# Second weight's conversion a step sooner, raw words two turns ahead, and k, q and v of batches 1 to 7 loaded from GpSimd's queue

## The chip, the cores and the metric

One core of a Trainium2 chip runs the kernel. The metric is the time of one execution in microseconds (us) on the device, lower is better. The kernel before was timed in three runs: 1645.82, 1646.19 and 1647.7, median 1646.19.

## The reference

```python
# q, k, v: (8 batches, 8 heads, 576 rows, 64), float32
q_s = softmax over the 64 features of each row of q
k_s = softmax over the 576 rows of each feature of k
kv  = einsum('bhsd,bhse->bhde', k_s, v)
att = einsum('bhsd,bhde->bhse', q_s, kv)
x = att.transpose(0, 2, 1, 3).reshape(4608, 512)
h = np.maximum(x @ w_in, 0.0)           # w_in 512 x 2048, w_out 2048 x 512
x = h * h @ w_out                       # first layer
h = x @ w_in2                           # second layer, own weights
out = (h / (1 + np.exp(-h))) @ w_out2   # silu
```

The four weights arrive as float64. q, k and v are float32.

## The kernel before

**Weights.** A float64 weight is read as raw 64-bit words (`raw`, loaded by `load_w`, L128 and L133, two DMAs a tile) and turned to float32 by hand (`to_f32`): ACT makes two activations (L143, L144), DVE four steps (L145, L148, L149, L152). Each weight has 8 tiles of 128 x 1024. Products are made in three matmuls from operands split in a high and a low half (`split`: ACT casts the high half at L117, DVE subtracts for the low half at L118; `mm3`, L187 to L189, gives high x high, high x low, low x high).

**Attention.** A `Pair` is two heads of one batch, 32 in all. `load` sets the padding of kr by a GpSimd memset (L241) and loads k (two DMAs, L235 and L239) and q (two: L235 and L239 for batches 0 and 1, L248 after them); `load_v` sets v's columns and padding by memsets (L257, L258) and loads v (three DMAs, L261 twice, L264). `k_max` takes the maximum on DVE (km, m: L269 to L271) and, across partitions, on GpSimd (L275, into mb); `k_sub` (L281) subtracts it, after which the buffer kr is free for the next pair's memset and load; `k_exp` (L288) is on ACT, `kv` (L296) and the transposed q times kv (`x`, matmuls named xp) on PE. For batches 2 to 7, q's own steps are `q_max` (L336 to L338), the exponential (L341), `q_norm` (L358 to L362), a transpose on DVE (L375) and the split of q into qh and ql.

**Prologue.** Batch 0's four pairs (`early`) run first, one step after the other in a loop over i, with loads on SP's and ACT's queues. `conv_first` converts the first tile of w_in (o = 0) and of w_out (o = 1); its generator is advanced once at step i = 2, and `run(conv)` takes the rest after the loop. The second of these, named w, feeds the first w_out product (matmuls named op). Its halves are the casts of `u` at L117 and L118.

**First layer.** Block 0 (512 tokens) goes through 16 steps f: hp = x @ w_in (L643), `relu2` (L632, L633) and the split into g, and op matmuls with w. Blocks 1 to 8 (j) take 8 turns each (m, one for each double tile i of the weights). A turn makes x @ w_in by a Strassen product of seven parts (matmuls L589, into a and c; additions at L601 to L624 on ACT and DVE into h), and the op matmuls of the turn before. Hooks in a turn advance the attention of the remaining 28 pairs (batches 1 to 7) by a phase. In the last turn of each j, `x_first` makes x for the next block (xt, L528 to L531, and the split in L118). SP loads in each turn the halves wah and wal of the weights' sums (L497).

**Second layer's weights.** `prepare` loads raw words of a tile (a step), converts them in the next step, and sends the result to DRAM (`wf`); from j = 2 on it is advanced in turns 0 to 5. After about 750 us the second layer begins: 6 steps of 8 turns.

**What sets the order.** Tile buffers are recycled: a pool tile with a tag (kr, v, q, mb) has one buffer, and the 19 large slots (`take`, `give`) are handed on in the order in which they come free. A scheduler orders the instructions of each engine by its own costs, so the order on an engine is not the order of the source. Each engine, and SP's and POOL's queue among them, runs its row in order. SP issues all loads but those early ones that ACT issues.

Of the kernel before, what the change touches and what calls it, by code (L numbers as in the profile page):

```python
# [11 lines left out]
U32 = mybir.dt.uint32  # L12
# [8 lines left out]
P = 128  # L21
# [9 lines left out]
def kernel(  # L31
# [13 lines left out]
    nc = tc.nc  # L45
    B, H, S, D = q.shape
# [4 lines left out]
    SM = S // TB * TB  # L51
    SL = S - SM
    NB = NT // TB
    SC = SM // P
# [7 lines left out]
    NP = NF // 2  # L62
# [4 lines left out]
    upool = ctx.enter_context(tc.tile_pool(name="u", bufs=2))  # L67
# [12 lines left out]
    def take(shape, dt, name):  # L80

        at = idle.pop(0)
        t = spool.tile(shape, dt, tag=f"s{at}", name=name)
        slot_of[id(t)] = (at, t)
        return t

    def give(*tiles):
        for t in tiles:
            idle.append(slot_of.pop(id(t))[0])

    def f32(t):
        return t.bitcast(F32)
# [18 lines left out]
    PW = 2 * NK * P  # L111
    wf = dpool.tile([2, NP, 2, P, PW], F32, name="wf")
# [8 lines left out]
    def load_w(l, i, o):  # L121

        raw = take([P, PW], U64, "raw")
        for e in range(2):
            f = slice((2 * i + e) * P, (2 * i + e + 1) * P)
            r = raw[:, e * NK * P:(e + 1) * NK * P]
            if o == 0:
                nc.sync.dma_start(  # L128
                    out=r.rearrange("p (k f) -> p k f", k=NK),
                    in_=(w_in1, w_in2)[l][:, f].rearrange("(k p) f -> p k f", p=P),  # L130
                )
            else:
                nc.sync.dma_start(out=r, in_=(w_out1, w_out2)[l][f, :])  # L133
        return raw

    def to_f32(u, raw, pin=False):

        words = raw.bitcast(U32).rearrange("p (n two) -> p n two", two=2)  # L140
        lo32, hi32 = words[:, :, 0], words[:, :, 1]
        keep = tc.keep_in_program_order if pin else lambda r: r
        keep(nc.scalar.activation(f32(lo32), lo32, AF.Copy, scale=2.0 ** -51, bias=2.0))  # L143
        keep(nc.scalar.activation(f32(u), f32(hi32), AF.Abs))  # L144
        nc.vector.tensor_scalar(  # L145
            out=f32(u), in0=f32(u), scalar1=EXP_LO, scalar2=EXP_HI, op0=ALU.max, op1=ALU.min
        )
        nc.vector.tensor_scalar(out=u, in0=u, scalar1=3, scalar2=None, op0=ALU.logical_shift_left)  # L148
        nc.vector.scalar_tensor_tensor(  # L149
            out=u, in0=hi32, scalar=0x80000000, in1=u, op0=ALU.bitwise_and, op1=ALU.bitwise_xor  # L150
        )
        nc.vector.tensor_tensor(out=u, in0=u, in1=lo32, op=ALU.add)  # L152
# [16 lines left out]

    def prepare():  # L170

        for i in range(NP):
            for o in range(2):
                raw = load_w(1, i, o)
                yield
                u = upool.tile([P, PW], U32, tag="u", name="u")
                to_f32(u, raw)
                give(raw)
                nc.sync.dma_start(out=wf[1, i, o], in_=f32(u))
                yield  # L180

    def run(steps):
# [18 lines left out]
    class Pair:  # L201
# [27 lines left out]
        def load(self):  # L229
            b, h0 = self.b, 2 * self.p  # L230
            self.kr = self.tile("kr", [P, 2, SC + 1, D], F32)
            self.q = self.tile("q", [P, 2, SC + 1, D] if self.natural else [P, S32, 32], F32)

            def rows(t, src, queue):
                queue.dma_start(  # L235
                    out=t[:, :, 0:SC].rearrange("p a c d -> p a (c d)"),
                    in_=src[b, h0:h0 + 2, 0:SM].rearrange("h (p c) d -> p h (c d)", p=P),
                )
                queue.dma_start(out=t[0:SL, :, SC], in_=src[b, h0:h0 + 2, SM:S].rearrange("h p d -> p h d"))  # L239

            nc.gpsimd.memset(self.kr[SL:P, :, SC], LEAST)  # L241
            rows(self.kr, k, nc.sync)
            if self.natural:
                nc.gpsimd.memset(self.q[SL:P, :, SC], 0.0)
                rows(self.q, q, nc.scalar if self.early else nc.sync)
            else:
                for dh in range(2):
                    nc.sync.dma_start(  # L248
                        out=self.q[64 * dh:64 * dh + 64],
                        in_=q[b, h0:h0 + 2, :, 32 * dh:32 * dh + 32].rearrange("h (s c) d -> (h s) c d", c=S32),  # L250
                    )

        def load_v(self):

            b, h0 = self.b, 2 * self.p
            self.v = self.tile("v", [P, SC + 1, 2, D + 1], F32)
            nc.gpsimd.memset(self.v[:, :, :, D:], 1.0)  # L257
            nc.gpsimd.memset(self.v[SL:P, SC, :, 0:D], 0.0)  # L258
            vv = self.v[:, :, :, 0:D]
            for a in range(2):  # L260
                nc.sync.dma_start(  # L261
                    out=vv[:, 0:SC, a], in_=v[b, h0 + a, 0:SM].rearrange("(p c) d -> p c d", p=P)
                )
            nc.sync.dma_start(out=vv[0:SL, SC], in_=v[b, h0:h0 + 2, SM:S].rearrange("h p d -> p h d"))  # L264

        def k_max(self):
            m = self.tile("m", [P, 2, D], F32)
# [363 lines left out]
    def relu2(h, src):  # L631
        nc.scalar.activation(h, src, AF.Relu)  # L632
        nc.scalar.activation(h, h, AF.Square)  # L633
        g = gpool.tile([P, 2, TB], F32R, tag="g", name="g")
        split(g[:, 0], g[:, 1], h)
        return g
# [93 lines left out]
    for i in range(NK + 2):  # L730
        a = early[i] if i < NK else None
        b = early[i - 1] if 1 <= i <= NK else None
        c = early[i - 2] if 2 <= i else None
        if a:
            a.q_exp()
            a.k_sub()
        if b:
            b.kv()
            b.q_norm()
            b.q_t()  # L740
        if i + 1 < NK:
            early[i + 1].k_max()
            early[i + 1].q_max()
        if b:
            b.kv_evac()
            b.q_split()
        if a:
            a.k_exp()
        if c:
            c.x_evac()  # L750
        if b:
            b.x()
        if i == 2:
            next(conv)
    run(conv)
    ahead = prepare()
# [30 lines left out]
    for j in range(1, NB):  # L787
        x, xs = xs, None
        for m, i in enumerate(turns[j - 1]):
            def hook(n):  # L790
                if (j, m, n) == (1, 0, 3):
                    wa.want(0)
                if n in (1, 6):
                    next(attend, None)
                    if j == 1 and (m, n) in ((1, 6), (3, 6)):
                        next(attend, None)
                if j < NB - 1:
                    if m == 4 and n == 0 and j == NB - 2:
                        XR[j + 1] = take([P, NK, TB], F32, "xr")
                        nc.sync.dma_start(out=XR[j + 1], in_=xld.rearrange("k p t -> p k t"))  # L800
                    if m == NP - 1:
                        if n == 0:
                            state["x"] = x_first(j + 1)
                            state["x"].split(2)
                        elif n == 4:
                            x.done(4)
                            state["x"].split(2)
                        elif n == 7:
                            x.done(NQ)
                            state["x"].split(3)  # L810
                else:
                    if m == 4 and n == 0:
                        state["raw"] = load_second(0)
                    elif m == 5 and n == 0:
                        state["x"] = x_second(state["raw"])
                        state["x"].split(2)
                    elif m == 6 and n == 0:
                        state["x"].split(1)
                    elif m == 7 and n == 0:
                        state["x"].split(1)  # L820
                    elif m == 7 and n == 4:
                        x.done(4)
                        state["x"].split(2)
                    elif m == 7 and n == 7:
                        x.done(NQ)
                        state["x"].split(1)

            state = {} if m == 0 else state
            h = hpool.tile([P, 2, TB], F32, tag="h", name="h")
            g = strassen(wa.tiles[0, i], x.x, TB // 2, h, lambda v: relu2(v, v), hook, (2, 2, 2))  # L830
            before = out_pair(j, m, i, g)
            t += 1
            wa.want(t)

            if j >= 2 and m < 6:
                next(ahead, None)
        xs = state["x"]
    run(ahead)
# [36 lines left out]
    for s in range(STEPS):  # L875
        x, state = xs, {}
        for m, i in enumerate(turns[NB - 1 + s]):
# [16 lines left out]
            h = lpool.tile([P, 2, TS], F32, tag="h", name="h")  # L894
# [37 lines left out]
```

## Time and profile before

| what | value |
|---|---|
| three runs | 1645.82, 1646.19, 1647.7 us |
| profiled execution, its own time | 1645.36 us |
| its span in the profile | 1643.5 us |
| granted TensorE clock, mean | 0.997 |
| ACT busy | 858.7 us (52%) |
| SP's queue (q1): packets, MB, share of 16 engines' span | 191152, 317.50, 58.2% |

The profile is of one execution. Busy times are sums over all instructions of an engine; PE is the matmul unit, PEld its weight load, DVE the vector engine, ACT the scalar engine, POOL GpSimd, SP the engine that issues most DMAs (SPq is its queue). A row of the time line is: start in us, duration, engine, line, operation, out<-in, shapes, count, and in brackets the idle time ahead of it with what ended it. A row by stretches of time is: the stretch and its length, busy time and count for PE, PEld, DVE, ACT and POOL, the granted clock of PE, the busy share of the DMA engines, GB/s. A row of waits is: engine, what waited, what for, then sum, count and longest. A row of groups gives the count, then the busy sum and mean ns of one, then the idle time ahead by what ended it. A row of DMA issues ends with the size and the median time from issue to landing.

### The profile page before, as it was taken

Reading aid. Unit: us, or ns where it says so; the run is one execution under the profiler, and the core shown is the slowest. Engines: PE = TensorE matmul, PEld = TensorE weight load, DVE = VectorE, ACT = ScalarE, POOL = GpSimd, SP = SyncE. Lnnn points to the kernel's source line nnn. Section 1 sums busy time; section 2 is a strip of 40 time slices with the busy share of each in tenths; the row PEclk is TensorE's granted clock in tenths of the full one; section 3 lists DMA queues with packets and bytes.
Section 4 is the critical chain, followed back from the end, with each engine's and each line's share of the span. In section 5 each row is a group of like instructions: output and inputs, shape, how many; then the busy total and the mean of one; then the engine's idle time right before and its main releaser. Section 6 shows DMA issues by size and latency. Waiting matters only on the chain.

```text
span 1643.5 us, 24901 instructions
## 1 busy us (share of the span) xinstructions
PE 1598.5 (97%) x9624; PEld 1394.2 (85%) x9624; DVE 979.3 (60%) x1708; ACT 858.7 (52%) x1529; POOL 55.4 (3%) x149
## 2 busy tenths in 40 slices
PE   4999999999999999999999999999999999999998
PEld 3567888888888888889998888998998998998997
DVE  7998896877858686643336765435435435435333
ACT  5866676666656665564556544324334334334332
POOL 2010000001000000000000000000000000000000
PEclk9999999999999999999999999999999999999999
DMA  8856767778685867554446875444444454454521
GB/s 258 285 161 201 232 201 236 224 244 243 172 266 153 256 207 240 191 192 167 159 164 246 325 277 186 158 170 170 150 180 168 143 189 165 136 205 161 180 95 39
DMA packets 193511, 320.41 MB, mean 195 GB/s; under 512 B 113264, under 2 KB 142960, under 8 KB 188528
## 3 DMA queue, kind: packets, MB, share of 16 engines
q1 hardware_dynamic: 191152, 317.50, 58.2%
q8 instruction: 76, 1.25, 0.3%
q10 hardware_dynamic: 2240, 1.31, 0.3%
q14 instruction: 43, 0.35, 0.1%
HBM read 248.51 MB, written 70.25 MB: 194 GB/s over the span
## 4 chain that ended last, share of the span: by engine, by line
PE 72%; DMA 5%; ACT 4%; DVE 3%; issue 1%; SPq 0%; POOL 0%; DVEq 0%; ACTq 0%; POOLq 0%
PE a L589 19%; PE c L589 14%; PE y L188 8%; PE y L189 8%; PE y L187 8%; PE op L188 5%; PE op L189 5%; PE op L187 5%; DMA raw<-in_moe_w_in_dram 2%; DMA raw<-in_moe_w_out_dram 2%; ACT h L632 1%; ACT raw L143 1%; ACT h L633 1%; PE xp L187 1%; DMA x1d<-o 0%
## 5 line engine op out<-in xcount | busy, mean ns | idle before, releaser
L589 PE MATMUL a<-x,wah 128*128 128x256 f32 (+1 forms) x1792 | 394.2, 307 | 5.6 <-ACT h L624 2.7
L589 PEld LDWEIGHTS a<-x,wah 128*128 128x128 f32 x1792 | 311.3, 189 | 36.6 <-ACT h L624 6.4
L589 PE MATMUL c<-x,wah 128*128 128x256 f32 (+1 forms) x1344 | 294.4, 306 | 1.9 <-DVE h L611 1.2
L589 PE MATMUL a<-x,wal 128*128 128x256 f32 (+1 forms) x896 | 273.9, 306 | 0.0
L187 PE MATMUL op<-g,w 128*128 128x512 f32 x576 | 231.0, 404 | 5.5 <-ACT w L117 5.4
L188 PE MATMUL op<-g,w 128*128 128x512 f32 x576 | 228.7, 397 | 0.3 <-DVE g L118 0.3
L589 PEld LDWEIGHTS c<-x,wah 128*128 128x128 f32 x1344 | 224.0, 190 | 3.7 <-DVE h L611 1.7
L189 PE MATMUL op<-g,w 128*128 128x512 f32 x576 | 225.7, 392 | 0.0
L189 PE MATMUL y<-wb,g 128*128 128x512 f32 x576 | 225.0, 391 | 0.0
L188 PE MATMUL y<-wb,g 128*128 128x512 f32 x576 | 224.8, 390 | 0.0
L187 PE MATMUL y<-wb,g 128*128 128x512 f32 x576 | 223.6, 390 | 0.5 <-ACT wb L117 0.5
L589 PE MATMUL c<-x,wal 128*128 128x256 f32 (+1 forms) x672 | 205.1, 305 | 0.0
L611 DVE TENSOR_TENSOR h<-c,h 128x256 f32<-128x256 f32 (+1 forms) x112 | 53.6, 478 | 250.4 <-PE c L589 248.8
L589 PEld LDWEIGHTS a<-x,wal 128*128 128x128 f32 x896 | 169.0, 189 | 0.6 <-DVE wal L118 0.6
L866 ACT ACTIVATE z<-h 128x768 f32<-128x768 f32 x96 | 80.5, 846 | 133.4 <-DVE h L619 132.3
L632 ACT ACTIVATE h<-h 128x512 f32<-128x512 f32 x128 | 80.9, 632 | 105.9 <-DVE h L619 104.8
L118 DVE TENSOR_TENSOR g<-h,g 128x512 fp32r<-128x512 f32 x128 | 88.3, 690 | 78.9 <-ACT g L117 78.5
L189 PEld LDWEIGHTS op<-g,w 128*128 128x128 f32 x576 | 108.9, 189 | 24.0 <-DVE w L118 0.5
L187 PEld LDWEIGHTS op<-g,w 128*128 128x128 f32 x576 | 109.6, 191 | 21.9 <-ACT w L117 5.5
L589 PEld LDWEIGHTS c<-x,wal 128*128 128x128 f32 x672 | 127.6, 190 | 0.0
L189 PEld LDWEIGHTS y<-wb,g 128*128 128x128 f32 x576 | 108.1, 188 | 22.4
L187 PEld LDWEIGHTS y<-wb,g 128*128 128x128 f32 x576 | 108.1, 188 | 22.0 <-ACT wb L117 0.8
(153 smaller groups left out, 2179.8 us busy)
## 6 DMA issues: line engine op xcount, KB each, us to landing
wah<-wad SPq DMA_DIRECT2D x72, 896.0 KB, 6.5
wal<-wad SPq DMA_DIRECT2D x72, 896.0 KB, 6.0
wb<-wbd SPq DMA_DIRECT2D x30, 1024.0 KB, 4.8
raw<-in_moe_w_in_dram SPq DMA_DIRECT2D x32, 512.0 KB, 5.9
raw<-in_moe_w_out_dram SPq DMA_DIRECT2D x32, 512.0 KB, 4.8
wad<-wah SPq DMA_DIRECT2D x16, 896.0 KB, 3.7
wad<-wal SPq DMA_DIRECT2D x16, 896.0 KB, 4.5
x1d<-o SPq DMA_DIRECT2D x18, 512.0 KB, 4.6
```

The costliest lines, as they stand in the source:

```text
L118: nc.vector.tensor_sub(lo, src, f32(hi))
L143: keep(nc.scalar.activation(f32(lo32), lo32, AF.Copy, scale=2.0 ** -51, bias=2.0))
L187: nc.tensor.matmul(ps, lh, rh, start=first, stop=False)
L188: nc.tensor.matmul(ps, lh, rl, start=False, stop=False)
L189: nc.tensor.matmul(ps, ll, rh, start=False, stop=last)
L589: nc.tensor.matmul(ps, l, r, start=first and c == 0 and n == 0, stop=c == 1 and n == 2, skip_group_check=True)
L611: nc.vector.tensor_add(h[:, 0, two], c, h[:, 0, two])
L632: nc.scalar.activation(h, src, AF.Relu)
L633: nc.scalar.activation(h, h, AF.Square)
L866: nc.scalar.activation(z, h, AF.Sigmoid)
```

## The change

Three edits. First, the generator of `conv_first` is advanced at step 3 of the prologue too, so the raw words of the first w_out tile are converted a step sooner. Second, `prepare` goes in groups of three tiles: the raw words of the next are loaded before those of the one ahead are converted, and the generator is advanced in turns 0, 2, 4 and 6 in place of 0 to 5. So a tile is converted two turns after its load, and up to two raw tiles are held. Third, k, q and v of batches 1 to 7 are issued by GpSimd: seven DMAs a pair, 196 in all, in place of SP. Lines after the diff's first piece have numbers that are 3 higher, and 4 higher from L261 on.

```diff
     def prepare():
-        for i in range(NP):
-            for o in range(2):
-                raw = load_w(1, i, o)
-                yield
-                u = upool.tile([P, PW], U32, tag="u", name="u")
-                to_f32(u, raw)
-                give(raw)
-                nc.sync.dma_start(out=wf[1, i, o], in_=f32(u))
+        todo = [(i, o) for i in range(NP) for o in range(2)]
+        for at in range(0, len(todo), 3):
+            raw = None
+            for i, o in todo[at:at + 3] + [(None, None)]:
+                done, raw = raw, None if i is None else (i, o, load_w(1, i, o))
+                if done:
+                    u = upool.tile([P, PW], U32, tag="u", name="u")
+                    to_f32(u, done[2])
+                    give(done[2])
+                    nc.sync.dma_start(out=wf[1, done[0], done[1]], in_=f32(u))
                 yield
...
-            rows(self.kr, k, nc.sync)
+            rows(self.kr, k, nc.sync if self.early else nc.gpsimd)
...
-                rows(self.q, q, nc.scalar if self.early else nc.sync)
+                rows(self.q, q, nc.scalar if self.early else nc.gpsimd)
             else:
                 for dh in range(2):
-                    nc.sync.dma_start(
+                    nc.gpsimd.dma_start(
...
+            queue = nc.sync if self.early else nc.gpsimd
             for a in range(2):
-                nc.sync.dma_start(
+                queue.dma_start(
...
-            nc.sync.dma_start(out=vv[0:SL, SC], ...)
+            queue.dma_start(out=vv[0:SL, SC], ...)
...
-        if i == 2:
+        if 2 <= i <= 3:
             next(conv)
...
-            if j >= 2 and m < 6:
+            if j >= 2 and m % 2 == 0:
                 next(ahead, None)
```

**DVE at the end of the prologue.** The rows below are those around the first split of g, which the first op matmuls need. u_380 is the buffer of the second weight before the change, u_340 the same after it; k_453 belongs to the first later pair, km_618 (from kr_523) to the second. Before:

```order
L281 TENSOR_TENSOR k_453<-kr_401,mb_420 128x640
L145 TENSOR_SCALAR u_380<-u_380 128x1024
L329 TENSOR_REDUCE qm_422<-q_402 128x10
L148 TENSOR_SCALAR u_380<-u_380 128x1024
L332 TENSOR_TENSOR q_402<-q_402,qm_422 128x640
L149 SCALAR_TENSOR_TENSOR u_380<-raw_157,u_380 128x1024
L118 TENSOR_TENSOR g_398<-r_395,g_398 128x512
L152 ISA u_380<-raw_157,u_380 128x2048
L344 TENSOR_REDUCE qs_426<-q_402 128x10
L145 TENSOR_SCALAR w32_434<-w32_434 128x1024
L118 TENSOR_TENSOR g_450<-r_447,g_450 128x512
L118 TENSOR_TENSOR w_387<-u_380,w_387 128x1024
```

After:

```order
L285 TENSOR_TENSOR k_453<-kr_401,mb_420 128x640
L118 TENSOR_TENSOR w_387<-u_340,w_387 128x1024
L336 TENSOR_TENSOR q_402<-q_402,qm_422 128x640
L145 TENSOR_SCALAR u_476<-u_476 128x1024
L148 TENSOR_SCALAR u_476<-u_476 128x1024
L307 TENSOR_SCALAR rec_518<-kvp_497 128x1
L273 TENSOR_TENSOR km_618<-kr_523 128x256
L149 SCALAR_TENSOR_TENSOR u_476<-raw_163,u_476 128x1024
L118 TENSOR_TENSOR g_398<-r_395,g_398 128x512
L348 TENSOR_REDUCE qs_426<-q_402 128x10
L152 ISA u_476<-raw_163,u_476 128x2048
```

The second weight's conversion (L145 to L152) has gone from between L281 and the splits to places ahead of these rows; its low half (w_387) is now made right behind the first later pair's subtraction. The low half of g_398 stands behind the km of the second later pair, which it stood ahead of.

**ACT at the same place.** r_395 is the first relu2, g_398 its high half. Before:

```order
L144 ACTIVATE u_380<-raw_157 128x1024
L632 ACTIVATE r_395<-hp_390 128x512
L288 ACTIVATE k_453<-k_453 128x640
L633 ACTIVATE r_395<-r_395 128x512
L632 ACTIVATE r_447<-hp_442 128x512
L117 CAST g_398<-r_395 128x512
L633 ACTIVATE r_447<-r_447 128x512
L341 ACTIVATE q_402<-q_402 128x640
L143 ACTIVATE raw_160<-raw_160 128x1024
L144 ACTIVATE w32_434<-raw_160 128x1024
L117 CAST g_450<-r_447 128x512
L117 CAST w_387<-u_380 128x1024
```

After:

```order
L144 ACTIVATE u_476<-raw_163 128x1024
L117 CAST w_387<-u_340 128x1024
L410 COPY xr_99<-xp_379 128x288
L410 COPY xr_99<-xp_381 128x224
L413 COPY big_126<-xp_381 128x64
L292 ACTIVATE k_453<-k_453 128x640
L414 DMA xld_95<-big_126 128x64
L636 ACTIVATE r_395<-hp_390 128x512
L143 ACTIVATE raw_428<-raw_428 128x1024
L637 ACTIVATE r_395<-r_395 128x512
L345 ACTIVATE q_402<-q_402 128x640
L117 CAST g_398<-r_395 128x512
```

The second weight's two activations (L143 and L144 of raw_157) and its high half (w_387) now stand ahead of the last early pair's x block; L143 of other raw words (raw_428) stands between the two activations of the first relu2.

**PE at the same place.** The first op matmuls; op0 to op3 are the four blocks of the result. Before:

```order
L296 MATMUL kvp_497<-v_409,k_453 64x65 x10
L187 MATMUL op0_460<-g_398,w_387 128x512
L188 MATMUL op0_460<-g_398,w_387 128x512
L187 MATMUL op1_464<-g_398,w_387 128x512
L189 MATMUL op0_460<-g_398,w_387 128x512
L188 MATMUL op1_464<-g_398,w_387 128x512
L189 MATMUL op1_464<-g_398,w_387 128x512
L187 MATMUL op2_468<-g_398,w_387 128x512
L188 MATMUL op2_468<-g_398,w_387 128x512
```

After:

```order
L300 MATMUL kvp_497<-v_409,k_453 64x65 x10
L190 MATMUL op0_460<-g_398,w_387 128x512
L190 MATMUL op1_464<-g_398,w_387 128x512
L190 MATMUL op2_468<-g_398,w_387 128x512
L190 MATMUL op3_472<-g_398,w_387 128x512
L191 MATMUL op0_460<-g_398,w_387 128x512
L192 MATMUL op0_460<-g_398,w_387 128x512
L191 MATMUL op1_464<-g_398,w_387 128x512
L192 MATMUL op1_464<-g_398,w_387 128x512
```

The four high x high matmuls now stand together ahead of those that need a low half.

**GpSimd in a turn.** One pair of batches 2 to 7, from a kr memset to the next. Before:

```order
L241 MEMSET kr 64x2x64
L257 MEMSET v 128x10
L258 MEMSET v 64x2x64
L275 ISA mb<-m 128x128
L241 MEMSET kr 64x2x64
```

After:

```order
L244 MEMSET kr 64x2x64
L238 DMA kr<-in_k_dram 128x2x256
L242 DMA kr<-in_k_dram 64x2x64
L251 DMA q<-in_q_dram 64x18x32 x2
L260 MEMSET v 128x10
L261 MEMSET v 64x2x64
L265 DMA v<-in_v_dram 128x4x64 x2
L268 DMA v<-in_v_dram 64x2x64
L279 ISA mb<-m 128x128
L244 MEMSET kr 64x2x64
```

All seven DMAs of the pair now stand in this row, v's three between the memsets of v and the next pair's all-reduce.

**DVE in the turn in which x is split.** One such turn, from the pair's subtraction to the next pair's km. Before:

```order
L281 TENSOR_TENSOR k<-kr,mb 128x640
L615 TENSOR_TENSOR h<-a,h 128x256
L358 TENSOR_REDUCE qs<-q 128x18
L619 TENSOR_TENSOR h<-c,h 128x256
L321 COPY qsu<-qs 64x18
L322 COPY qsu<-qs 64x18
L360 SCALAR_TENSOR_TENSOR qs<-qs,qsu 128x18
L361 RECIPROCAL qs<-qs 128x18
L362 TENSOR_TENSOR q<-q,qs 128x576
L269 TENSOR_TENSOR km<-kr 128x256
```

After:

```order
L285 TENSOR_TENSOR k<-kr,mb 128x640
L619 TENSOR_TENSOR h<-a,h 128x256
L118 TENSOR_TENSOR ql<-qt,qh 128x576
L623 TENSOR_TENSOR h<-c,h 128x256
L379 STREAM_TRANSPOSE qt<-q 128x576
L273 TENSOR_TENSOR km<-kr 128x256
```

The next pair's km has moved up: q's sum and normalization no longer stand between the subtraction and it.

More of the change, by code (lines that the diff above doesn't have):

```diff
@@ L259, in load_v @@
             vv = self.v[:, :, :, 0:D]
+            queue = nc.sync if self.early else nc.gpsimd
             for a in range(2):
-                nc.sync.dma_start(
+                queue.dma_start(
                     out=vv[:, 0:SC, a], in_=v[b, h0 + a, 0:SM].rearrange("(p c) d -> p c d", p=P)
                 )
-            nc.sync.dma_start(out=vv[0:SL, SC], in_=v[b, h0:h0 + 2, SM:S].rearrange("h p d -> p h d"))
+            queue.dma_start(out=vv[0:SL, SC], in_=v[b, h0:h0 + 2, SM:S].rearrange("h p d -> p h d"))
         def k_max(self):
```

## Prediction

> **What bounds the kernel now.** I read the page first, then the busy table by stretches of time, then what PE waited for, then the time line around each of those waits.
>
> ```profile
> PE 1598.5 (97%) x9624; PEld 1394.2 (85%) x9624; DVE 979.3 (60%) x1708; ACT 858.7 (52%) x1529; POOL 55.4 (3%) x149
> ...
> 20.00:40.00 20.00, 16.72 (x121) 10.00 (x121) 15.09 (x36) 14.25 (x32) 1.73 (x4) 1.00 0.91 289
> 40.00:60.00 20.00, 14.89 (x43) 9.48 (x44) 20.00 (x28) 17.27 (x22) 0.84 (x2) 0.83 0.91 286
> ...
> 1600.00:1643.50 43.50, 38.48 (x188) 33.84 (x187) 12.91 (x17) 11.88 (x19) 0.00 (x0) 0.98 0.10 37
> ```
>
> PE is the bound: its idle time is 1643.5 - 1598.5 = 45.0 us of the span, 5.0 of it (43.50 - 38.48) at the very end. The change touches nothing after the first layer (about 750 us), so it can only win PE's holes before that, and the clock where a hole costs it. In 40 to 60 the granted clock is 0.83. The holes by cause:
>
> ```profile
> DVE h L611 <- PE c L589: 248.8, 68, 6.5
> ...
> ACT raw L143 <- DMA raw<-in_moe_w_in_dram: 18.2, 7, 4.2
> ...
> PE kvp L296 <- ACT big L341: 16.7, 1, 16.7
> ...
> DVE k L281 <- POOL mb L275: 12.5, 19, 0.9
> DVE km L269 <- DMA kr<-in_k_dram: 12.1, 7, 3.2
> ...
> PE op L187 <- ACT w L117: 5.4, 1, 5.4
> PE xp L187 <- ACT kvh L117: 5.3, 6, 1.2
> ...
> PE a L589 <- ACT h L624: 2.7, 5, 0.9
> ```
>
> Each row names who waits for whom, then the sum, the count and the longest. Of PE's four, the 16.7 us is the first attention pair before any matmul; its loads stay on SP and ACT. The 5.4 is the wait for the second weight, the 5.3 and 2.7 lie in the turns. ACT and DVE wait for raw words and for k; whether PE pays is seen only at each place.
>
> **Part 1, the second weight's conversion.** Its steps (L143, L144 on ACT, L145 to L152 on DVE, the two halves by L117, L118) end ahead of the first w_out1 matmul:
>
> ```profile
> 30.68 0.43 SPq L235 DMA_DIRECT2D kr<-in_k_dram  x1
> 31.18 0.34 DVE L306 SCALAR_TENSOR_TENSOR big<-kvp,big,mask_n 128x128 f32<-128x128 f32 x1
> 32.79 0.58 ACT L380 COPY big<-qt 128x512 f32<-128x512 f32 x1 [3.07 <-PE qt L369]
> 34.70 0.42 DVE L269 TENSOR_TENSOR km<-kr 128x256 f32<-128x256 f32 x1 [3.18 <-DMA kr<-in_k_dram]
> 36.61 0.82 DVE L281 TENSOR_TENSOR k<-kr,mb 128x640 f32<-128x640 f32 x1 [0.83 <-POOL mb L275]
> 36.64 1.15 ACT L144 ACTIVATE u<-raw 128x1024 f32<-128x1024 f32 x1
> 37.69 0.57 ACT L632 ACTIVATE r<-hp 128x512 f32<-128x512 f32 x1
> 44.01 1.05 ACT L117 CAST w<-u 128x1024 fp32r<-128x1024 f32 x1
> 45.11 0.80 PE L187 MATMUL op<-g,w 128*128 128x512 f32 x1 [5.37 <-ACT w L117]
> ...
> 44.00:46.00 2.00, 0.89 (x2) 0.80 (x3) 2.00 (x4) 2.00 (x3) 0.00 (x0) 0.51 1.23 252
> ...
> 48.00:50.00 2.00, 2.00 (x6) 1.60 (x5) 2.00 (x3) 2.00 (x3) 0.00 (x0) 0.50 0.25 79
> 50.00:55.00 5.00, 5.00 (x15) 2.70 (x15) 5.00 (x9) 2.43 (x3) 0.64 (x1) 0.91 0.74 210
> ...
> L145 DVE TENSOR_SCALAR u<-u 128x1024 f32<-128x1024 f32 x24 | 16.6, 691 | 18.0 <-ACT u L144 18.0
> L152 DVE CUSTOM_DVE_ANT_0 u<-raw,u 128x2048 uint16<-128x2048 uint16 x24 | 29.3, 1223 | 0.0
> ```
>
> PE stands 5.37 us and then runs at half clock from 45.1 to about 50.9 (0.91 over the 5 us from 50 is 0.9 us at a half): (50.9 - 45.1) x 0.5 = 2.9 us more. So this place holds 5.4 + 2.9 = 8.3 us, and no more. The room for the earlier conversion is there: ACT is idle 3.07 us ahead of 32.79 and DVE 3.18 ahead of 34.70. The conversion takes 2 x 1.15 = 2.3 us of ACT and, with each of its four DVE steps at one of the last two rows (two at 0.69, two at 1.22), 3.8 us of DVE. It is not free, for DVE's queue now has those 3.8 us ahead of the last pair's L306 (before, it ended at 31.5). That ends near 31.5 + 3.8 = 35.3, and the x block and the first hp matmul need it. The first relu2 (L632) could then start at about 38, as now. But ACT's queue now puts L143, L633, L341 and the cast of g behind it: 38 + 0.57 + 1.15 + three steps of about 0.65 = 41.7. So the four hi-hi matmuls that now open PE's row can start at 41.7 instead of 45.1.
>
> The next matmul, L188, wants the low half of g. In DVE's new row that stands behind the L269 of the second later pair, and so behind that pair's load of k, which GpSimd may issue only when L281 of the pair ahead has read the buffer. L281 stays near 36.6 to 37.4. With 0.2 us for the memset, one issue (about 1 us, below) and a landing of 4.0 (30.68 to 34.70, the load that L269 waited for here), L269 runs at 42.6, and after it stand 0.4 + 1.2 + 0.7 us: low half at 44.9. PE then stops from 42.7 to 44.9. It has done 4 of the 12 matmuls by then and goes on 0.2 us ahead of before, with 0.9 us of work in hand: 1.1 us gained. The clock is not told by a row: a hole of 5.37 gave 0.50, and here there are two of about 2. I take half of its 2.9. Part 1: -1.1 - 1.5 = -2.6, between -8.3 (nothing waits) and +2 (the load of k lands 5 us later, as at 368.97 below, and the clock falls as before).
>
> The Trainium skill, "TensorE: Matmul & The Clock Gate", Part 1: The HAM clock gate, says that the array falls to half rate after about one idle window of some 3.4 us. By it two holes of about 2 us keep full rate, and Part 1 would be -4.0 instead of -2.6; the 0.50 after 5.37 us agrees with it.
>
> **Part 2, k, q and v on GpSimd's queue, and raw words earlier.** The six waits of PE's xp matmul are four of 1.19 us (4.76 of the 5.3), at like places of four j in a row, and two of some 0.25. The first of the four:
>
> ```profile
> 361.52 0.83 DVE L281 TENSOR_TENSOR k<-kr,mb 128x640 f32<-128x640 f32 x1 [0.91 <-POOL mb L275]
> ...
> 367.76 1.11 SPq L128 DMA_DIRECT2D raw<-in_moe_w_in_dram  x2
> 368.97 0.46 SPq L235 DMA_DIRECT2D kr<-in_k_dram  x1
> 374.96 1.16 ACT L143 ACTIVATE raw<-raw 128x1024 f32<-128x1024 uint32 x1 [1.78 <-DMA raw<-in_moe_w_in_dram]
> 376.10 0.43 DVE L269 TENSOR_TENSOR km<-kr 128x256 f32<-128x256 f32 x1 [2.07 <-DMA kr<-in_k_dram]
> 383.63 0.40 PE L187 MATMUL xp<-qh,kvh 128*128 128x288 f32 x1 [1.19 <-ACT kvh L117]
> ...
> 368.97 7.11 DMA kr<-in_k_dram
> ```
>
> SP issues k only at 368.97, behind the raw words and what they waited for, though L281 had read the buffer by 361.52 + 0.83 = 362.3; it lands 7.11 us later. DVE stands 2.07 us, then has the conversion and the kv block to do, and PE's xp matmul comes 1.19 us late. On GpSimd k goes out at about 362.6, so it is in place by 370, and the raw words have two more turns: both waits end, what is next is DVE's own work, and 4 x 1.19 = 4.8 us of PE are free. The other holes of the turns (L624 2.7, the two small xp waits 0.5) I leave as they are: a floor of 0 and a top of 4.8 + 3.2 = 8.0.
>
> What is added is GpSimd's time and the order on it. No row shows a DMA issued by POOL. POOL is in order: in each of 28 pairs 7 issues (k 2, q 2, v 3) now stand there, v's three between the memset that waits for the kv matmuls and the all-reduce of the next pair's maximum.
>
> ```profile
> L275 POOL PARTITION_ALL_REDUCE mb<-m x28 | 29.1, 1039 | 175.0 <-DVE m L271 163.2 <-DVE qs L360 8.7 <-DVE qm L337 3.1
> L258 POOL MEMSET v<- 64x128 f32 x28 | 7.3, 260 | 1.6
> ...
> q<-in_q_dram SPq DMA_DIRECT2D x48, 144.0 KB, 4.4
> kr<-in_k_dram SPq DMA_DIRECT2D x28, 256.0 KB, 4.9
> ...
> 449.82 0.70 DVE L148 TENSOR_SCALAR u<-u 128x1024 uint32<-128x1024 uint32 x1
> ...
> 449.90 0.76 POOL L258 MEMSET v<- 64x128 f32 x1
> ```
>
> An issue costs between SP's 0.46 (the k row) and 4.4, if POOL were held till q has landed. I take 1.04, the all-reduce, which is nearest: a program on POOL over 128 partitions. The all-reduce sat idle 163.2 / 24 = 6.8 us for its input, so three issues (3.1 us) fit; the seven with memsets and all-reduce are 9 us, and 28 pairs in the some 700 us of the first layer have 25 us each. What the cover doesn't hold is the new order on DVE: the next pair's L269 now stands right behind L281 and the transpose (L375), with 1.7 to 2.0 us of DVE work between, where there were 2.5 to 5.9. k is there 0.2 + 1.04 + (4.0 to 4.9) = 5.2 to 6.1 us after L281. In most turns L611 and its wait for PE (248.8 us / 68 = 3.7 each, in the list of waits above) lie between, and cover it. In the turn in which x is split they don't. So I let DVE stand 3 to 4 us (5.2 to 6.1 less 1.7 to 2.0) there once in each j of 2 to 7; at 2.07 us of standing PE paid 1.19, so 6 x 0.5 = 3 us is my price, less than 1.19 each because L615 and L619, with waits of their own, still lie between, and the bounds are 0 and 6 x 2 = 12. SP's loss of 28 x 7 = 196 issues is costed at nothing more: of PE's 45.0 us idle the four rows above and the end hold 35.1, and none of them is for wah or wal, which SP also loads.
>
> **The sum.** -2.6 - 4.8 + 3.0 = -4.4 us against the profiled execution's own 1645.36: 1641.0. The median shown is 0.8 above it: 1641.8. The bounds: -8.3 - 8.0 = -16.3, and +2 + 12 = +14, without the rivals.
>
> **The rivals.** *GpSimd too slow*: at 2 us an issue the three of v and the memset take 6.3 us of the 6.8 on average, and at 3 us 9.3: each all-reduce 2.5 us late, L281 and all behind it on DVE late with it, and at 1.19 for 2.07 PE loses 1.4 x 24 = 34 us: 1641.8 + 34 = 1676. It decides from about 2.2 us, where 0.3 us a pair and the later k (1.2 us) eat the gain. For it: a load of q has 1152 runs of 128 B; against it: the only issues shown, SP's of k, are of 0.43 and 0.46. In the prologue the seven loads of the first pair also stand ahead of the last early pair's all-reduce.
>
> *Held by DVE*: the memset that takes 0.26 on average took 0.76 beside a TENSOR_SCALAR of 0.70. If issues are held so, each of the 16 conversions, whose two TENSOR_SCALARs now stand right at v's memset, delays v's issues by up to 1.4 us: 3.1 + 1.4 is still under 6.8, but not where a pair follows the last more closely than on average, which I put at 8 places, 1 us each and 0.6 of it PE's: 5 us, so 1641.8 + 5 = 1646.8, no change. The Trainium skill, "SBUF — State Buffer", SBUF: two separate sides, has this rule: descriptors of a GpSimd DMA can't be written while a VectorE operation holds the shared port pair. The stretched memset agrees with it.
>
> *Hidden anyway*: the four xp holes close but DVE's stand at L269 opens as many, and Part 1 gives the clock's part alone: 1644 to 1647. *All of it*: both holes close fully, 1646.2 - 16 = 1630.
>
> **How the numbers follow.** Forecast, some of the gain kept (1635 to 1643): 0.45. All of it (1629 to 1635): 0.10. Hidden, or held by DVE (1643 to 1649.5): 0.18. GpSimd too slow, or a late k in the prologue with it (1649.5 to 1680, half of it below 1662): 0.27. The range 1629 to 1662 leaves out 0.14. Faster than 1642.9 (0.2%, about what a measurement tells from no change) 0.55, slower than 1649.5 0.27, the rest 0.18; the forecast case alone gives 1635 to 1643.
>
> **What would show it.** Right: no PE wait for w at the first op matmul over 2.5 us and a clock near 1.00 from 44 to 50; ACT's wait for raw words near 0; no 1.19 us xp waits in j of 3 to 6; POOL's DMA rows near 1 us. Wrong: DVE's wait for kr above 30 us or for mb above 40 us in all (12.5 now), POOL's issues of 2 us and more, or PE's idle time above 45 us before 750.

## The result and the profile after

The changed kernel took 1708.83 us (median of 4 runs, 1704.32 to 1712.67) where the kernel before took 1646.01 (4 runs, 1643.75 to 1647.70). The ratio is 1.0389, 95% interval 1.0375 to 1.0404: 62.8 us slower. The forecast was 1641.8, range 1629 to 1662.

The head of the page after, and PE's and DVE's largest waits for data or for each other (engine, what waited, what for, sum, count, longest):

```profile
PE 1618.5 (95%) x9624; PEld 1407.0 (82%) x9624; DVE 982.5 (58%) x1708; ACT 864.4 (51%) x1529; POOL 198.7 (12%) x345
```

```profile
PE a L593 <- ACT h L628: 19.1, 11, 3.5
PE a L593 <- DVE h L619: 17.6, 6, 4.6
PE kvp L300 <- ACT big L345: 16.9, 1, 16.9
PE c L593 <- DVE h L615: 6.9, 6, 3.0
PE op L191 <- DVE g L118: 5.4, 2, 3.7
```

```profile
DVE km L273 <- DMA kr<-in_k_dram: 55.8, 18, 6.7
...
DVE qm L339 <- DMA q<-in_q_dram: 17.1, 8, 4.9
...
DVE k L285 <- POOL mb L279: 12.2, 17, 0.9
```

PE's idle time is 1706.8 - 1618.5 = 88.3 us, 43.3 more than before. Its busy time is 20.0 us longer for the same 9624 matmuls; the mean granted clock is 0.987 where it was 0.997. The two make up the 63.3 us between the spans. DVE, which waited 12.1 us for k and never long for q, now waits 55.8 + 17.1 = 72.9. PE's new holes in the turns are nearly all waits for Strassen's additions: L628, L619 and L615 hold 43.6 us of it, where they held 5.2 before.

One such place shows how the two belong together. The time line of the changed kernel, cut to k and what stands behind it (SPq is SP's queue):

```profile
420.68 0.83 DVE L285 TENSOR_TENSOR k<-kr,mb 128x640 f32<-128x640 f32 x1 [0.91 <-POOL mb L279]
...
421.64 0.38 SPq L501 DMA_DIRECT2D wah<-wad  x1
...
421.71 0.73 POOL L238 DMA_DIRECT2D kr<-in_k_dram  x1
...
429.97 0.42 DVE L273 TENSOR_TENSOR km<-kr 128x256 f32<-128x256 f32 x1 [6.67 <-DMA kr<-in_k_dram]
...
430.64 0.42 DVE L619 TENSOR_TENSOR h<-a,h 128x256 f32<-128x256 f32 x1
...
431.11 0.80 PE L593 MATMUL a<-x,wah 128*128 128x256 f32 x2 [4.61 <-DVE h L619]
```

k goes out 0.20 us after the subtraction has freed its buffer, but 0.07 us behind a weight load of 896 KB that SP has just issued, and is there only 8.3 us later. DVE reaches km after 1.6 us and stands 6.67 us at it. The addition L619, whose input was ready, stands behind km on DVE's row, so PE stands 4.61 us. The clock falls behind such a hole, as the granted clock (the third number from the end) shows around this place and around 401, where PE stood 3.20 us:

```profile
400.00:405.00 5.00, 3.33 (x12) 2.77 (x13) 2.14 (x6) 2.73 (x5) 0.00 (x0) 0.75 0.49 113
...
430.00:435.00 5.00, 3.89 (x12) 3.41 (x13) 2.91 (x8) 3.41 (x6) 0.00 (x0) 0.50 0.30 75
435.00:440.00 5.00, 5.00 (x31) 4.63 (x31) 3.17 (x9) 2.34 (x6) 0.00 (x0) 0.84 0.79 320
```

The Trainium skill, "TensorE: Matmul & The Clock Gate", Part 1: The HAM clock gate, has the array fall to half rate after an idle window of some 3.4 us. The 0.50 behind a hole of 4.61 agrees with it; behind the hole of 3.20, a little shorter than that window, the granted clock was 0.52 from 404 to 406 as well.

Where the 62.8 us lie: the first product of the turns (L589 before, L593 now) starts at 143.21 before and at 154.23 now, so 11.0 us are lost in the prologue and block 0; from there to the end it is 1500.3 us before and 1552.6 now, 52.3 us, all of it ahead of the last attention pair's xp matmul (692.1 before, 756.9 now). What makes up the 11.0 us stays open: PE's two stops ahead of the first op products (1.83 and 3.66, see Part 1 below) come to no more than the 5.37 that they replace.

### The profile page after: what moved, and what is told of

Same layout as the page of the kernel before. It is cut to its first block, busy times and chain, and to the rows that moved or that the text cites. A ratio compares the mean times of both kernels' runs of the same rounds, so it can differ in the third digit from the quotient of the medians.

```text
span 1706.8 us, 24895 instructions
## 1 busy us (share of the span) xinstructions
PE 1618.5 (95%) x9624; PEld 1407.0 (82%) x9624; DVE 982.5 (58%) x1708; ACT 864.4 (51%) x1529; POOL 198.7 (12%) x345
## 2 busy tenths in 40 slices
DMA packets 100775, 320.41 MB, mean 188 GB/s; under 512 B 21616, under 2 KB 43888, under 8 KB 95792
## 3 DMA queue, kind: packets, MB, share of 16 engines
q0 software_dynamic: 10240, 24.79, 5.4%
## 4 chain that ended last, share of the span: by engine, by line
PE 53%; DMA 2%; ACT 2%; DVE 1%; issue 0%; SPq 0%; POOL 0%; DVEq 0%; ACTq 0%; POOLq 0%
PE a L593 14%; PE c L593 11%; PE y L191 8%; PE y L192 8%; PE y L190 8%; PE op L191 2%; PE op L190 2%; PE op L192 2%; DMA c<-wf 1%; DMA x1d<-o 0%; DMA raw<-in_moe_w_out_dram 0%; DMA raw<-in_moe_w_in_dram 0%; DMA kr<-in_k_dram 0%; ACT h L637 0%; ACT wah L117 0%
## 5 line engine op out<-in xcount | busy, mean ns | idle before, releaser
L593 PE MATMUL a<-x,wah 128*128 128x256 f32 (+1 forms) x1792 | 397.6, 309 | 38.0 <-ACT h L628 19.1
L593 PEld LDWEIGHTS a<-x,wah 128*128 128x128 f32 x1792 | 313.8, 191 | 71.8 <-ACT h L628 23.8
L593 PE MATMUL c<-x,wah 128*128 128x256 f32 (+1 forms) x1344 | 296.3, 307 | 7.0 <-DVE h L615 6.9
L593 PE MATMUL a<-x,wal 128*128 128x256 f32 (+1 forms) x896 | 275.2, 307 | 0.0
L191 PE MATMUL op<-g,w 128*128 128x512 f32 x576 | 232.6, 404 | 5.5 <-DVE g L118 5.4
L190 PE MATMUL op<-g,w 128*128 128x512 f32 x576 | 234.0, 409 | 1.8 <-ACT g L117 1.8
L593 PEld LDWEIGHTS c<-x,wah 128*128 128x128 f32 x1344 | 225.1, 191 | 9.9 <-DVE h L615 8.7
L192 PE MATMUL op<-g,w 128*128 128x512 f32 x576 | 228.6, 397 | 0.0
L593 PE MATMUL c<-x,wal 128*128 128x256 f32 (+1 forms) x672 | 205.9, 306 | 0.0
L615 DVE TENSOR_TENSOR h<-c,h 128x256 f32<-128x256 f32 (+1 forms) x112 | 53.5, 478 | 241.3 <-PE c L593 240.8
L593 PEld LDWEIGHTS a<-x,wal 128*128 128x128 f32 x896 | 170.6, 190 | 0.0
L192 PEld LDWEIGHTS op<-g,w 128*128 128x128 f32 x576 | 111.1, 193 | 24.6
L191 PEld LDWEIGHTS op<-g,w 128*128 128x128 f32 x576 | 111.8, 194 | 21.5 <-DVE g L118 6.9
L593 PEld LDWEIGHTS c<-x,wal 128*128 128x128 f32 x672 | 128.3, 191 | 0.0
```

What stands on the lines that cost most here:

```text
L190: nc.tensor.matmul(ps, lh, rh, start=first, stop=False)
L191: nc.tensor.matmul(ps, lh, rl, start=False, stop=False)
L192: nc.tensor.matmul(ps, ll, rh, start=False, stop=last)
L593: nc.tensor.matmul(ps, l, r, start=first and c == 0 and n == 0, stop=c == 1 and n == 2, skip_group_check=True)
L615: nc.vector.tensor_add(h[:, 0, two], c, h[:, 0, two])
```

## The experiments

The theories at the start were *row* (what costs is that the scheduler moved the steps that read k and q up on DVE's row), *queue* (GpSimd's queue itself brings the data late) and *raw words* (the second edit costs). Later a fourth stood in for *queue*: *shared engines* (k is late where another queue's weight load was issued just ahead of it).

**The first two edits alone**, k, q and v on SP as before.

> The first two edits alone; k, q and v stay on SP. Theory 'row' (the loss is km's place on DVE's row, which the third edit moved): DVE waits for k as before, 12 us, so 1638 to 1648 us. Theory 'queue' (the loss is that GpSimd's queue brings k and q late): the same, 1638 to 1648. Theory 'raw words' (two raw tiles held and conversions in turns 2, 4, 6 hit the split of x): 1660 or more.

1645.47 us, ratio 1.0004 (0.9992 to 1.0015): no difference. *Raw words* falls. The waits that the forecast had promised did go:

```profile
PE a L592 <- ACT h L627: 4.5, 5, 1.7
PE xp L190 <- ACT kvh L117: 1.6, 5, 0.6
PE op L190 <- ACT g L117: 1.5, 1, 1.5
```

The xp waits fell from 5.3 to 1.6 and the wait ahead of the first op matmul from 5.4 to 1.5. Others came: ACT's waits for raw words rose from 18.2 + 11.6 to 27.4 + 20.2 us. From the first product of the turns (144.57) to the end this profile takes 1496.9 us, 3.4 less than before; up to there it takes 1.4 more. Both are within what the runs of one kernel differ by (1641.99 to 1648.51 here).

**The third edit alone** (GpSimd's loads, without the first two).

> The third edit alone. 'Row' and 'queue': most of the 62 us stays, 1695 to 1715. 'Raw words': 1640 to 1655.

1711.69 us, ratio 1.0404 (1.0380 to 1.0428). All of the loss is in this edit.

**The first edit alone.**

> The first edit alone. My part 1 without GpSimd's load of k in the way: PE's wait for the second weight (5.4 us) and the half clock behind it (2.9 us) go, or shrink to 2 us: 1638 to 1644. If the wait only moves to the low half of g: 1645 to 1647.

1644.24 us, ratio 1.0004 (0.9990 to 1.0018). The hole of 5.37 us closed here too (first op matmul at 42.19 in place of 45.11, and the clock stays at 1.00 from 40 to 60), and yet the first product of the turns starts at 147.71 in place of 143.21. The profiled execution took 1649.28 us, 5 more than the median, so that much delay is not the median run's. But it shows where the gain can go: PE stands at places further on where it did not stand before. The largest of them, 2.4 us at 112.89:

```profile
PE qt L372 <- DVE m L306: 2.6, 2, 2.4
```

The busy table of the kernel before says how full DVE is there:

```profile
40.00:60.00 20.00, 14.89 (x43) 9.48 (x44) 20.00 (x28) 17.27 (x22) 0.84 (x2) 0.83 0.91 286
60.00:80.00 20.00, 20.00 (x67) 12.26 (x65) 19.03 (x29) 15.73 (x24) 1.10 (x3) 1.00 0.87 285
80.00:100.00 20.00, 20.00 (x88) 12.65 (x87) 19.40 (x30) 17.77 (x26) 2.71 (x4) 1.00 0.78 252
100.00:120.00 20.00, 20.00 (x88) 12.64 (x87) 20.00 (x30) 10.94 (x19) 2.06 (x4) 1.00 0.30 87
```

The third busy time is DVE's: 78.4 of the 80 us. PE's, the first, is 20.00 too from 60 on, so neither engine has room. A conversion that is made sooner takes the place of other work on DVE, and PE can come to wait somewhere else. This is argued from these rows, not shown: no run took work off DVE.

**km pinned.** All three edits; the first step of km is held behind what the program wrote before it on DVE.

```diff
-            nc.vector.tensor_max(t, self.kr[:, :, 0:2], self.kr[:, :, 2:4])
+            r = nc.vector.tensor_max(t, self.kr[:, :, 0:2], self.kr[:, :, 2:4])
+            if self.b >= 1:
+                tc.keep_in_program_order(r)
```

> All three edits, and the first step of km of every later pair (its maximum over k) is held behind all that the program wrote before it on DVE, so it stands 19 or more rows behind the subtraction in place of 3 or 4; GpSimd still issues all loads. 'Row': DVE's wait for k falls from 55.8 to under 10 us, the additions no longer stand behind it, 1635 to 1655. 'Queue': k and q are as late as before, 1680 or more.

1704.27 us, ratio 1.0358 (1.0343 to 1.0374). As stated, *row* missed. Its waits show why:

```profile
DVE qm L341 <- DMA q<-in_q_dram: 39.4, 14, 7.1
...
DVE km L273 <- DMA kr<-in_k_dram: 2.7, 1, 2.7
```

The wait for k went from 55.8 to 2.7 and that for q rose from 17.1 to 39.4: qm (maximum over q) stands 5 to 9 rows behind the transpose that frees q's buffer in the steady turns, where it stood 7 to 27 behind before the change, and took k's part. But the two waits together fell from 72.9 to 42.1 us and the time by only 4.6: what DVE stands is not what PE loses, and the waits alone don't price a run.

**Both pinned, on GpSimd and on SP.** The same pin on qm as well; once with all three edits, once with the first two (k, q, v on SP). In the steady turns km and qm stand at the same places on DVE's row in both. The rest of the rows is not quite the same: on DVE the steps behind one pair's kv in four (rec, m, kvl) stand some rows earlier with SP, and on ACT some copies and casts change places. So the pair differs in the queue and in little else.

```diff
-            nc.vector.reduce_max(m, self.q, axis=AX.X)
+            r = nc.vector.reduce_max(m, self.q, axis=AX.X)
+            tc.keep_in_program_order(r)
```

> All three edits, and both first steps of a later pair on DVE, km (maximum over k) and qm (maximum over q), held behind all that the program wrote before them; GpSimd still issues k, q and v. 'Row' (the loss is where the scheduler puts the steps that read k and q on DVE's row): DVE's waits for k and for q fall under 10 us together, 1640 to 1665. 'Queue' (GpSimd's queue itself brings the data late): 1685 or more, with DVE still waiting for q.

> The control of the run ahead: the first two edits and the same two pins, but SP issues k, q and v. DVE's row in the steady turns is the same, so only the queue differs. 'Row': within 10 us of the run ahead. 'Queue': 30 us or more faster than it.

On GpSimd 1670.07 us, ratio 1.0153 (1.0130 to 1.0176); on SP 1654.97, ratio 1.0059 (1.0044 to 1.0074). So with GpSimd's queue untouched, the two pins take 38.8 of the 62.8 us back: what DVE's row does is the larger part. The queue costs 15.1 us with km and qm at the same places, between what the two theories had said, and the pins themselves some 10. DVE's waits for k and q are down to 2.7 and 2.2 us in the first. What is left in the tables of issues are later landings; that these, and not the few rows that differ, make the 15.1 us is not shown. For v and q, on GpSimd and then on SP (the last column is the median from issue to landing, us):

```profile
v<-in_v_dram POOLq DMA_DIRECT2D x56, 128.0 KB, 6.9
q<-in_q_dram POOLq DMA_DIRECT2D x48, 144.0 KB, 6.4
```

```profile
v<-in_v_dram SPq DMA_DIRECT2D x56, 128.0 KB, 3.5
q<-in_q_dram SPq DMA_DIRECT2D x48, 144.0 KB, 4.2
```

**k on SP; q on SP.** All three edits, with one of the three tensors back on SP.

```diff
-            rows(self.kr, k, nc.sync if self.early else nc.gpsimd)
+            rows(self.kr, k, nc.sync)
```

> All three edits, but k goes back to SP; q and v stay on GpSimd. The scheduler still puts km 3 to 10 rows behind the subtraction and qm 4 to 7 behind the transpose. 'Row': DVE still waits for k, 20 us or more, though SP issues it, 1665 to 1700. 'Queue': the wait for k goes, that for q stays, 1645 to 1665.

> All three edits, but q goes back to SP; k and v stay on GpSimd. The scheduler puts qm 13 to 26 rows behind the transpose, as before the change, and km 2 to 8 rows behind the subtraction. 'Row': the wait for q goes, that for k stays at 25 us or more, 1660 to 1690. 'Queue': the same for k; 1665 to 1690.

k on SP: 1693.27 us, ratio 1.0278 (1.0249 to 1.0307); DVE waits 10.6 us for k and 46.6 for q. The time is within *row*'s range, but the wait for k isn't: *row* had said 20 us or more, *queue* none. q on SP: 1698.86, ratio 1.0323 (1.0306 to 1.0341); 46.4 us for k, none for q, and a time a little over both ranges. The pace of k is seen where a weight load is near. First k on SP, then k on GpSimd (q on SP):

```profile
613.23 0.82 DVE L285 TENSOR_TENSOR k<-kr,mb 128x640 f32<-128x640 f32 x1 [0.91 <-POOL mb L279]
...
614.08 0.38 SPq L238 DMA_DIRECT2D kr<-in_k_dram  x1
...
615.31 0.54 SPq L501 DMA_DIRECT2D wah<-wad  x1
...
618.42 0.43 DVE L273 TENSOR_TENSOR km<-kr 128x256 f32<-128x256 f32 x1 [1.05 <-DMA kr<-in_k_dram]
```

```profile
490.49 0.43 SPq L501 DMA_DIRECT2D wah<-wad  x1
...
490.61 0.83 DVE L285 TENSOR_TENSOR k<-kr,mb 128x640 f32<-128x640 f32 x1 [0.24 <-POOL mb L279]
...
491.64 0.73 POOL L238 DMA_DIRECT2D kr<-in_k_dram  x1
...
498.38 0.43 DVE L273 TENSOR_TENSOR km<-kr 128x256 f32<-128x256 f32 x1 [4.06 <-DMA kr<-in_k_dram]
```

On SP, wah stands behind k on the queue, so it goes out 1.2 us after k, and k is there in 4.3 us. Off SP, wah goes out 1.15 us ahead of k, and k takes 6.7. This gave the fourth theory. It is put too narrowly, as the same run with q on SP shows: for four pairs (k issued at 351.35, 460.10, 567.45 and 671.73) km ran 5.7 to 6.4 us after the issue with no wah within 5 us ahead. There wal, q and v, issued 2.7 to 5.5 us ahead, were still under way.

**k from ACT's queue.** All three edits; k of batches 1 to 7 is issued by ACT, whose queue the page lists as `hardware_dynamic`, like SP's; GpSimd's is `software_dynamic`.

```diff
-            rows(self.kr, k, nc.sync if self.early else nc.gpsimd)
+            rows(self.kr, k, nc.sync if self.early else nc.scalar)
```

> All three edits, but k of batches 1 to 7 is issued from ACT's queue; q and v stay on GpSimd. DVE's row is nearly that of the changed kernel (km 4 rows behind the subtraction). Theory 'shared engines' (k lands late where SP, no longer held behind k, issues a weight load of 896 KB up to 1.2 us ahead of it from another queue): landings of 6 us and more with such a load in front, near 3 us without, as on GpSimd; DVE waits for k 30 us or more; 1685 to 1715. Theory 'GpSimd's queue is slow by itself': k lands in 3 to 4 us everywhere, the wait falls under 15 us, 1660 to 1690.

1701.76 us, ratio 1.0343 (1.0315 to 1.0371), 44.5 us of waiting for k. Two places of its time line, with a weight load just ahead and without:

```profile
411.52 0.38 SPq L501 DMA_DIRECT2D wah<-wad  x1
...
411.60 0.39 ACTq L238 DMA_DIRECT2D kr<-in_k_dram  x1
...
419.36 0.43 DVE L273 TENSOR_TENSOR km<-kr 128x256 f32<-128x256 f32 x1 [4.60 <-DMA kr<-in_k_dram]
...
443.64 0.37 ACTq L238 DMA_DIRECT2D kr<-in_k_dram  x1
...
446.50 0.43 DVE L273 TENSOR_TENSOR km<-kr 128x256 f32<-128x256 f32 x1 [0.76 <-DMA kr<-in_k_dram]
```

7.8 us in the one, 2.9 in the other, without GpSimd in either. Over the 16 pairs of this run from 300 on, km runs 6.1 to 11.1 us after the issue where wah was issued up to 1.1 us ahead (8 pairs) and 2.8 to 3.7 in seven of the other eight; in the eighth, at 352.06, k landed after 5.5 us beside wal, v and q, with no wah near. In the changed kernel it is the same, over 16 pairs: 5.8 to 8.3 us in the eight where wah stands within 1.2 us of k, and 3.1 to 3.3 in the eight where it doesn't. So GpSimd isn't what makes k land late; loads still under way are. The Trainium skill, "DMA: Bandwidth & Descriptors", Issuing engines are not separate DMA queues, says that DMAs of all issuing engines run on the same 16 engines and interleave. These rows agree.

One thing more is in the two first profiles. In the kernel before, k landed late as well: from 350 us on, in the seven pairs where raw words stood up to 1.4 us ahead of it on SP's queue, km ran 5.3 to 7.5 us after the issue, and SP issued k there only 5.7 to 6.8 us after the subtraction. So k was in place 11.5 to 13.7 us after the subtraction there. In the changed kernel the same seven pairs are the late ones, and k is in place at most 8.4 us after the subtraction. Where it is late, k came no later with the change; km came to stand nearer to the subtraction.

**v alone on GpSimd.** The first two edits, and v's three loads a pair on GpSimd; k and q on SP.

> The first two edits, and of the third only v on GpSimd; k and q are issued by SP. The scheduler leaves km 3 to 14 and qm 13 to 26 rows behind what frees their buffers. 'Row' with 'shared engines': waits for k and q under 10 us together, 1643 to 1660. If v's later landing (6.1 us for 3.2) or POOL's three issues ahead of the all-reduce cost by themselves: 1665 or more.

1651.28 us, ratio 1.0053 (1.0028 to 1.0077), 8.5 us of waiting for k and 2.5 for q, a little over the 10 us expected. In time as *row* with *shared engines* had it: v's later landing (5.6 us here) and the three issues ahead of the all-reduce cost little by themselves, some 8 us by the ratio of the first two edits alone (1.0004).

**k's small load as a gate.** Against the run with q on SP, one DMA a pair is moved: the small one of k's two goes back to SP, where it waits for the subtraction and holds wah behind it. The large one stays on GpSimd.

```diff
-                queue.dma_start(out=t[0:SL, :, SC], in_=src[b, h0:h0 + 2, SM:S]...)
+                (tail or queue).dma_start(out=t[0:SL, :, SC], in_=src[b, h0:h0 + 2, SM:S]...)
...
-            rows(self.kr, k, nc.sync if self.early else nc.gpsimd)
+            rows(self.kr, k, nc.sync if self.early else nc.gpsimd, nc.sync)
```

> The run with q on SP (k and v on GpSimd, 1698.9 us), with one DMA a pair moved: the small one of k's two (32 KB) goes back to SP, where it waits for the subtraction and so holds the weight loads behind it; the large one (256 KB) stays on GpSimd. DVE's row is the same but for one place. 'Shared engines' (what costs is the weight load that SP, no longer held, issues ahead of k): SP's wah is issued behind k, k's large DMA lands in 3 to 4.5 us in the turns where the small one stands ahead of wah, DVE waits for k under 20 us in place of 46, 1650 to 1670. If k's lateness belongs to GpSimd's queue: no change, 1690 or more.

1670.49 us, ratio 1.0140 (1.0115 to 1.0166): 28.4 us faster than the run it differs from, by 32 KB a pair that changed its queue. It ends half a us above the range expected, and the wait for k fell less far, from 46.4 to 30.4 us. With q on SP, and then here:

```profile
DVE km L273 <- DMA kr<-in_k_dram: 46.4, 14, 4.1
```

```profile
DVE km L273 <- DMA kr<-in_k_dram: 30.4, 15, 4.0
```

wah is now issued 0.5 or 2.6 us behind k, and k takes 3.3 to 6.5 us there: a load issued half a microsecond later still runs beside k. In one place of four, wal and v, issued 2.7 to 5.9 us ahead, are still under way, and k takes up to 5.3.

**v from ACT's queue.** The run with both pins and all three edits, with v issued by ACT; a single run, for v's landing.

```diff
-            queue = nc.sync if self.early else nc.gpsimd
+            queue = nc.sync if self.early else nc.scalar
```

> All three edits with km and qm pinned (the run of 1670.1 us), but v of batches 1 to 7 is issued by ACT, which may stand at its waits. Only the landing of v counts here. If v lands late from GpSimd because other queues' loads run beside it: from ACT too, 5 us or more from issue to landing in the median. If the lateness belongs to GpSimd's queue: near SP's 3.2 to 3.5 us.

```profile
v<-in_v_dram ACTq DMA_DIRECT2D x56, 128.0 KB, 7.4
```

7.4 us, against 6.9 from GpSimd and 3.5 from SP, with the same pins. v is late from ACT's queue too, so its lateness is not GpSimd's own. The kernel before has it even on SP: from 400 us on v's first load took 4.8 to 5.8 us in the three places where wal had been issued 0.56 us ahead of it, and 2.5 to 4.0 in the other nine. In the changed kernel, from 380 us on, wal goes out within 0.3 us of v in all 14 places. The time of this one run, 1668.56 us (a run of the kernel before on the same chip: 1648.31), is near that of the run on GpSimd.

## Why the prediction was wrong

**The step that failed** is the cover of the late k in Part 2: "In most turns L611 and its wait for PE ... lie between, and cover it", and with it the price of 3 us with the bounds "0 and 6 x 2 = 12". The mechanism stood in the prediction, place and all (L269 right behind L281, k not there yet); it was counted for the turn in which x is split and no other. There it came to 1.07, 1.21 and 1.17 us in the last three pairs of that kind, less than the 3 to 4 forecast, with no weight load near; from 390 us on the stands of 3.7 to 6.7 us are all in other turns. The trace after has 18 stands at km and 8 at qm. The forecast's own sign of being wrong, a wait for kr above 30 us, came: 55.8. No rival reached 1708.8 either; the farthest went to 1680. Three things were mis-sized. The cover: in the place shown above L615 does lie between L285 and km, but it found its input ready and didn't wait, and DVE stood 6.67 us. The landing: 4.0 to 4.9 us were taken as if every pair's were the same, though the forecast's own row had 7.11 behind raw words; the median after is 4.6, but from 300 us on it was 3.1 to 3.3 without a weight load near and 5.8 to 8.3 with one. And the price per stand, 0.5 us, came from a hole of 1.19 behind a stand of 2.07; stands of 5.32 and 6.67 cost PE 3.20 and 4.61 us and the clock besides, which the prediction's own row of 5.37 us at 0.50 should have told.

**"SP's loss ... is costed at nothing more"** was the other error. That PE waited neither for wah nor for wal was right. But SP's wait for the subtraction, ahead of k, had also kept the next weight load off the engines till k was out: before, in the pairs from 360 us on where wah is near, it goes out 1.8 to 3.4 us behind k. Taking k off SP set wah free, and it went first.

**q** was not priced at all beyond its issues. The scheduler moved qm up as well (17.1 us, 39.4 once km was pinned).

**GpSimd too slow** gave the nearest time of the rivals (1676) by the wrong cause. The issues are short, and the all-reduce is no later than before (12.2 us of waiting in place of 12.5):

```profile
L265 POOL DMA_DIRECT2D v<-in_v_dram x56 | 42.8, 768 | 2.8 <-issue 0.3
L251 POOL DMA_DIRECT2D q<-in_q_dram x48 | 41.3, 865 | 95.1 <-DVE qt L379 68.4 <-ACT g L117 10.7 <-DVE kvl L118 5.6
...
L238 POOL DMA_DIRECT2D kr<-in_k_dram x28 | 20.4, 727 | 0.0
...
L242 POOL DMA_DIRECT2D kr<-in_k_dram x28 | 17.5, 627 | 0.3 <-issue 0.3
```

**Held by DVE** happened, and hardly cost: of the 196 issues five took over 0.1 us more than others of their kind, four of them beside a TENSOR_SCALAR of DVE. v's last at 596.66, the longest, took 1.03 us in place of 0.61, with L145 running from 596.88. The five stretches come to 1.3 us in all, where this rival had up to 1.4 for each of 16 conversions.

**Part 1**: the low half of g behind the second later pair's km was rightly named, and its size not: that km stood 4.16 us and ran at 49.41, not at 42.6, and PE's second stop was 3.66 us in place of 2.2. The first op matmul came at 46.63, behind a first stop of 1.83, and not at 41.7. Alone, without GpSimd, the edit closed its hole and gained nothing in time. The forecast had priced the hole as if nothing behind it could take the gain. DVE's full rows up to 120 us say that something can; that DVE is what takes it is not shown.

**Part 2's gain**: the four holes of 1.19 us do go with the second edit (5.3 to 1.6 us), for which GpSimd wasn't needed. The time shows nothing that can be told from no change. ACT's wait for raw words, which the forecast had near 0, is 18.0 and 10.8 us in the changed kernel (18.2 and 11.6 before).

## What to carry to other kernels

Moving a load to another engine's queue changed two orders here besides its own: the scheduler's, which put the load's consumer earlier on an engine that runs in order, and that of the queue left behind, where a wait had been holding back other traffic. Before such a move, look at what stands behind the load on its old queue and at what stands behind its consumer on the consumer's engine; here both mattered. Where the scheduler is too hopeful about a load, pinning the consumer can pay: with the loads on SP the pins cost some 10 us, with the loads on GpSimd they saved 38.8.

## What was not expected of the hardware

With k, q and v on GpSimd the page counts 100775 DMA packets where it had 193511, for the same 320.41 MB. Its rows of queues say where they went:

```profile
DMA packets 100775, 320.41 MB, mean 188 GB/s; under 512 B 21616, under 2 KB 43888, under 8 KB 95792
...
q0 software_dynamic: 10240, 24.79, 5.4%
```

GpSimd's 24.79 MB went in 10240 packets, 2.4 KB each, though q's runs are of 128 B. Fewer packets didn't make the loads faster. From issue to landing, in the median, k took 4.6 us in place of 4.9, q 4.5 in place of 4.4 and v 6.1 in place of 3.2:

```profile
kr<-in_k_dram POOLq DMA_DIRECT2D x28, 256.0 KB, 4.6
v<-in_v_dram POOLq DMA_DIRECT2D x56, 128.0 KB, 6.1
q<-in_q_dram POOLq DMA_DIRECT2D x48, 144.0 KB, 4.5
```

That v is slow was not GpSimd's doing alone, as the run with v on ACT shows.
